# Score tiles of a causal attention in half-array pieces, with the masked quarter of each diagonal block given to another block's scores

## The chip, the cores and the metric

One core of one Trainium2 chip runs the whole program in one launch. The metric is device time in microseconds: 447.69 us, the median of three runs (447.2 to 447.72).

TensorE multiplies matrices into PSUM, here one tile of 8 banks of 128 partitions x 512 fp32. VectorE and ScalarE read PSUM, GpSimd doesn't. SyncE issues most transfers. Each engine works through its own instructions in the order in which the program was written, and semaphores join the engines.

## What is computed

`x` is [1, 2048, 576], bfloat16. The first half of the block is an attention with a compressive memory over four segments of 512 tokens, 32 heads of 18 channels each; the second is a dense layer with GELU, 576 to 4608 and back.

```python
ar = jnp.arange(L)                                   # L = 512
mask = (ar[:, None] < ar[None, :]) * -1000000000.0
for s in range(N):                                   # N = 4 segments
    qs, ks, vs = q[:, :, s], k[:, :, s], v[:, :, s]
    p = _softmax(jnp.einsum('bhqd,bhkd->bhqk', qs, ks) * scale + mask)
    a_dot = jnp.einsum('bhqk,bhkd->bhqd', p, vs)
    pq = phi(qs)
    a_mem = einsum(pq, M) / (einsum(pq, z) + 1e-06)
    outs.append(g * a_mem + (1.0 - g) * a_dot)
    M, z = M + einsum(phi(ks), vs), z + sum(phi(ks))
h = x + attention(_layernorm(x)) @ wo
out = h + gelu(_layernorm(h) @ w1 + b1) @ w2 + b2
```

A query sees only keys at or before it in its segment. So of each 512 x 512 score matrix only the key-query pairs on and below the diagonal count.

## The kernel before

**An order written out by hand.** The program is built as a graph of small operations (`Graph.add`), each with an engine, a cost and a list of those it must follow. A large table, `TIMETABLE`, gives each operation its place: the key is a stage tag and a name ("A1mask": the masks of the attention in segment 1), the letters say which engine (p TensorE, a ScalarE, d VectorE, g GpSimd, s SyncE), and the numbers are places in one order over all engines. `schedule` sorts by these places, hands out buffers, and the instructions are written in that order. So an operation that is not ready holds up all that come behind it on its engine. The costs in `add` are the planner's, used to choose buffers; they are not times of the chip.

**Stages.** X is the first layernorm of a segment, P the three projections, A the attention, M the memory update, B the output projection with the second layernorm, C the first dense product (L1301, in segment 0 L1338), D the second (L1388). TensorE's work of C and D of one segment is laid between that of A of the next. In B, a tile's two halves `Po` and `Ro` run fused (L819, ten matmuls of 128 rows) where they follow each other directly, or else as 10 and 8 matmuls of 64 rows (L793).

**The scores.** A group is four heads; a segment has eight groups. Scores are kept transposed, keys on the partitions and queries along the free axis. Heads have 18 channels, padded to 32, so the four heads of a group use the four 32-row strips of the array at once, each writing its own PSUM bank (`tile_position=(32 * i, 0)`). Key tile `kt` (128 keys) needs queries from `kt * 128` to 512: 512, 384, 256 and 128 columns. A score step fills 512 columns of four banks, and one exponential of 128 x 2048 empties them into a buffer of `pt` (five buffers). In segments 1 to 3 (`stage_A`) five steps serve two groups (`STEPS`): 20 steps a segment, 60 in all, scored at L1163 and exponentiated at L1167. In segment 0 (`stage_A0`) 20 steps are made of other units (L1002, L1005), six of them of four diagonal blocks of 128 columns.

The first 128 columns of every such unit are the diagonal block: half of it is above the diagonal and set to zero by a mask after the exponential. One mask a key tile, by VectorE as a product with a triangle (L1176) or by GpSimd as a select (L1178); in stage 0 two blocks at once (L1015, L1018). The quarter with the upper 64 keys and the lower 64 queries of a diagonal block is void as a whole.

**The values.** Per group, `val` (L1189; L1034 in stage 0) multiplies the four buffers with the values, 16 matmuls on four column tiles of 32, each reading all 128 keys. Then the result is transposed (L1197), divided and combined with the memory's part: `rg` on GpSimd (L1125), `eg` on ScalarE (L1123) and `pq` on VectorE (L1127) make phi(q) in buffers `e` and `r`, and `mem` (L1134 in the full array, L1137 in column tiles) multiplies it.

**Changes of tiling.** Scores use row strips, values column strips, the projections and the first dense product 64-row halves, the rest the full array.

**What else shares the engines.** GpSimd also does rstd of each layernorm (L714, L715), the clips and part of the combining; VectorE and ScalarE share the evictions of PSUM (L630, L634, L1306, L1314, L1316). `warm_up` (L644) runs full-array products of zeros before the first data is there.

Of the kernel before, what the change touches and what calls it, by code (L numbers as in the profile page):

```python
# [318 lines left out]
}  # L319
# [141 lines left out]
def kernel(  # L461
# [11 lines left out]
    nc = tc.nc  # L473
# [1076 lines left out]
```

## Time and profile before

| | |
|---|---|
| time, median of 3 | 447.69 us |
| profiled execution, first to last instruction | 444.7 us |
| TensorE busy | 431.7 us, 97% |
| weight loads | 278.3 us, 63% |
| VectorE, ScalarE, GpSimd busy | 291.2, 296.7, 179.3 us |
| granted TensorE clock | 0.999 |
| exponentials of the scores | 60 of 1.878 us and 20 of 1.880 us |
| score matmuls (L1163, L1002) | 384 and 224 |
| value matmuls (L1189, L1034) | 384 and 224 |

The time is taken around the execution, the span from its first instruction to its last; the profiled execution has only its span. A row of the timeline reads: start, length, engine, line, operation, what it writes and reads, how many, and in brackets the idle time of the engine before it and what ended it. A matmul's length contains the way through the array, so lengths of neighbours overlap: sixteen matmuls that end 0.72 us after their start may let the next one begin after 0.55. A row of the waits reads: who waited, for whom, total, times, longest.

### The profile page before, as it was taken

What the parts mean: (1) busy time and instruction counts of PE and PEld (TensorE: products, weight loads), DVE (VectorE), ACT (ScalarE), POOL (GpSimd) and SP (SyncE); (2) the same over time, 40 slices, a digit from 0 to 9 for tenths busy, and PEclk for the clock granted to TensorE, in tenths of its full rate; (3) what the DMA queues carried; (4) which work ended last, traced back from release to release, by engine and by line L of the source; (5) the groups of instructions that cost most, each with busy time, mean ns of one, the idle gap of its engine ahead of it and who ended that gap; (6) DMA issues with size and microseconds to landing.
All of it is one profiled execution on the core that took longest, in us unless ns stands there. A gap on an engine that the chain in (4) does not pass through costs nothing.

```text
span 444.7 us, 12623 instructions
## 1 busy us (share of the span) xinstructions
PE 431.7 (97%) x5355; PEld 278.3 (63%) x5355; DVE 291.2 (65%) x636; ACT 296.7 (67%) x269; POOL 179.3 (40%) x312
## 2 busy tenths in 40 slices
PE   8888999998999999999999999999999999999997
PEld 5666677765676776664445766654457775446775
DVE  5889888999899988867777987837765121010011
ACT  5999999999878798686798966752684002556000
POOL 5776756457748435734236559440011000000010
PEclk9999999999999999999999999999999999999999
DMA  6779989999999945693863355805463461550030
GB/s 208 204 250 246 271 264 279 228 228 244 236 257 348 315 152 166 175 242 69 245 190 52 107 146 161 201 2 153 131 210 111 101 171 39 169 194 1 1 107 28
DMA packets 85274, 76.73 MB, mean 173 GB/s; under 512 B 62945, under 2 KB 72545, under 8 KB 85217
## 3 DMA queue, kind: packets, MB, share of 16 engines
q1 hardware_dynamic: 85072, 75.83, 63.3%
q8 instruction: 42, 0.69, 0.7%
q10 hardware_dynamic: 144, 0.09, 0.1%
q14 instruction: 16, 0.12, 0.1%
HBM read 42.08 MB, written 18.87 MB: 137 GB/s over the span
## 4 chain that ended last, share of the span: by engine, by line
PE 75%; DVE 7%; DMA 6%; ACT 6%; POOL 2%; issue 2%; SPq 1%; POOLq 0%; DVEq 0%; ACTq 0%
PE bank L1388 27%; PE bank L1301 21%; PE bank L835 9%; PE bank L1338 6%; DMA w1g<-in_B_w_dram 4%; PE bank L1163 3%; ACT hT L1355 3%; PE bank L1189 3%; PE bank L793 2%; DMA x<-in_A_x_dram 2%; ACT pt L1167 1%; PE bank L1002 1%; PE bank L819 1%; DVE ln L710 1%; POOL pt L1178 1%
## 5 line engine op out<-in xcount | busy, mean ns | idle before, releaser
L1167 ACT ACTIVATE pt<-bank 128x2048 bf16<-128x2048 f32 x60 | 112.7, 1878 | 30.4 <-PE bank L1163 25.1
L1388 PEld LDWEIGHTS <-hT 128*128 128x128 bf16 x1152 | 110.2, 98 | 34.5 <-issue 7.0
L1301 PE MATMUL bank<-xreg,w1g 64*128 64x512 bf16 x972 | 108.0, 376 | 0.2 <-DMA w1g<-in_B_w_dram 0.2
L1301 PEld LDWEIGHTS <-w1g 64*128 64x128 bf16 x972 | 46.2, 94 | 57.1 <-issue 2.3
L1388 PE MATMUL bank<-w,hT 128*128 128x288 bf16 x576 | 78.3, 286 | 0.0
L1388 PE MATMUL bank<-w_lo,hT 128*128 128x288 bf16 x576 | 78.0, 286 | 0.0
L835 PE MATMUL bank<-hT,xreg 64*128 64x288 bf16 x864 | 58.0, 283 | 1.1 <-DVE qk_pad L634 0.6
L1306 ACT ACTIVATE hT<-bank,b_col 128x512 bf16<-128x512 f32 x36 | 22.5, 689 | 46.0 <-PE bank L1301 46.0
L1178 POOL TENSOR_SCALAR_AFFINE_SELECT pt<-pt 128x512 bf16<-128x512 bf16 x58 | 42.0, 737 | 27.1 <-ACT pt L1167 26.9
L835 PEld LDWEIGHTS <-xreg 64*128 64x128 bf16 x864 | 41.6, 94 | 14.3 <-issue 5.0
L1400 DVE TENSOR_TENSOR ot<-bank,hc 128x288 bf16<-128x288 f32 x32 | 13.8, 448 | 52.2 <-PE bank L1388 51.1
L1316 DVE TENSOR_SCALAR hT<-bank,b_col 128x512 bf16<-128x512 f32 x49 | 34.9, 742 | 18.6 <-PE bank L1301 18.5
L1374 POOL TENSOR_TENSOR hc<-hc,b_bc 128x576 f32<-128x576 f32 x9 | 11.7, 1297 | 82.0 <-DMA hc<-hd 82.0
L1005 ACT ACTIVATE pt<-bank 128x2048 bf16<-128x2048 f32 x20 | 37.6, 1880 | 2.8 <-PE bank L1002 2.1
L1338 PE MATMUL bank<-xreg,w1g 64*128 64x256 bf16 x648 | 38.3, 269 | 0.6 <-DMA w1g<-in_B_w_dram 0.6
L1338 PEld LDWEIGHTS <-w1g 64*128 64x128 bf16 x648 | 31.3, 94 | 6.4 <-issue 2.7
L1374 DVE TENSOR_TENSOR hc<-hc,b_bc 128x576 f32<-128x576 f32 x7 | 5.6, 817 | 43.8 <-DMA hc<-hd 43.8
L1321 ACT ACTIVATE hT<-hT 128x8192 bf16<-128x8192 bf16 (+2 forms) x6 | 31.8, 5321 | 1.7 <-DVE hT L1316 1.6
L1314 ACT ACTIVATE hT<-bank,b_col 128x512 bf16<-128x512 f32 x23 | 15.1, 685 | 21.9 <-PE bank L1301 21.6
L1176 DVE TENSOR_TENSOR pt<-pt,tri 128x512 bf16<-128x512 bf16 x38 | 21.5, 569 | 4.7 <-ACT pt L1167 4.7
L1163 PE MATMUL bank<-qk 32*128 32x512 bf16 (+3 forms) x384 | 23.8, 300 | 0.2
L1349 DVE TENSOR_TENSOR hT<-bank,b_col 128x512 bf16<-128x512 f32 x32 | 21.0, 681 | 3.8 <-PE bank L1338 3.4
(117 smaller groups left out, 564.1 us busy)
## 6 DMA issues: line engine op xcount, KB each, us to landing
w1g<-in_B_w_dram SPq DMA_DIRECT2D x41, 576.0 KB, 5.0
qkd<-qk_pad SPq DMA_DIRECT2D x15, 512.0 KB, 3.9
hd<-h SPq DMA_DIRECT2D x16, 288.0 KB, 3.9
hc<-hd SPq DMA_DIRECT2D x16, 288.0 KB, 3.6
w_lo<-in_B_w_dram SPq DMA_DIRECT2D x3, 864.0 KB, 7.0
w<-in_B_w_dram SPq DMA_DIRECT2D x3, 864.0 KB, 11.1
xb<-in_A_x_dram SPq DMA_DIRECT2D x16, 144.0 KB, 4.2
x2d<-xn SPq DMA_DIRECT2D x14, 160.0 KB, 2.9
```

The costliest lines, as they stand in the source:

```text
L835: nc.tensor.matmul(out=out, lhsT=xTb.t[r, k, ts], rhs=wt[r, k, :], start=(k == 0), stop=(k == ND - 1))
L1005: ex = add(ps, {"act": 1.88}, lambda e: nc.scalar.activation(out=pt.t[:], in_=st.t[:], func=ACT.Exp, scale=scale), [sc], pt, [st], table=" ...
L1163: nc.tensor.matmul(out=st.t[:, i, off:off + n_], lhsT=qk[rows, 1, kt * P:(kt + 1) * P], rhs=qk[rows, 0, kt * P:L], start=True, stop=True, ...
L1167: ex = add(ps, {"act": 1.88}, lambda e, st=st, pt=pt: nc.scalar.activation(out=pt.t[:], in_=st.t[:], func=ACT.Exp, scale=scale), [sc], pt, ...
L1176: nc.vector.tensor_tensor(out=blk, in0=blk, in1=tri[:].unsqueeze(1).to_broadcast([P, 4, P]), op=ALU.mult)
L1178: nc.gpsimd.affine_select(out=blk, in_=blk, pattern=[[0, 4], [1, P]], compare_op=ALU.is_ge, fill=0.0, base=0, channel_multiplier=-1)
L1301: nc.tensor.matmul(out=cc[w].t[:], lhsT=w1.t[rows, k, q, :], rhs=x2T[s].t[rows, k, :], start=(k == 0), stop=(k == ND - 1))
L1306: ready_f[f + w] = [add(pf - 12, {"act": 0.68}, lambda e, f=f, w=w, cc=cc: nc.scalar.activation(out=hT[:, :, f + w, :], in_=cc[w].t[:].rea ...
L1316: nc.vector.tensor_scalar(out=dst, in0=src, scalar1=b, scalar2=None, op0=ALU.add)
L1321: ge = add(2.9, {"act": 0.42 * (f1 - f0) + 0.2}, lambda e, f0=f0, f1=f1: nc.scalar.activation(out=hT[:, :, f0:f1, :], in_=hT[:, :, f0:f1, ...
L1338: nc.tensor.matmul(out=cc[w].t[:, q * 2 * P:(q + 1) * 2 * P], lhsT=w1.t[rows, k, q, :], rhs=x2T[s].t[rows, k, ts], start=(k == 0), stop=(k ...
L1388: nc.tensor.matmul(out=c.t[:, 0:HALF], lhsT=hT[:, tl // 2, f, (tl % 2) * P:(tl % 2 + 1) * P], rhs=w2_c[ch][:, f - ch * WCH, hf * HALF:(hf ...
```

## The change

- `STEPS` now has nine steps for four groups; each unit is (group, key tile, first query, queries, place). 18 steps a segment.
- `halves` makes each unit of two kinds of matmul, both with 64 keys: one for the lower 64 keys at tile position (32 i, 0), one for the upper at (32 i, 64). For an even key tile, the upper half's first 64 columns, the void quarter, take upper-half-placed scores of the next key tile (its first 64 keys against its first 64 queries); the remaining columns take the unit's own upper keys. The next, odd key tile then leaves out its first 64 queries.
- After the exponential, `drop` copies that quarter, times a triangle, from partitions 64 to 127 to partitions 0 to 63 of a new buffer `low` (one buffer, its upper partitions zero from the start). Only then may `cut` mask the diagonal block, which also zeroes the void quarter. Odd tiles are masked in one operation as two 64 x 64 triangles.
- `val` reads odd key tiles in pieces, the first from `low`: 24 or 28 matmuls a group.
- In stage 0 the six steps of four diagonal blocks are packed likewise into 384 of 512 columns; the two of the first kind keep the quarter in the free columns of their own `pt` buffer.
- `r` has one buffer for two. The warm-up products write other banks. A memset on GpSimd zeroes the upper partitions once.
- The timetable is new throughout: order, and for some operations the engine.

```diff
-    "A1mask": "d456 g466 g515 g495 g474 g547 g537 g545 g620 g585 d572 d602 g645 g633 g643 d616 g661 d681 g672 g674 d705 d686 d712 g713 d744 g757 g756 g762 "
-        "d755 d766 g730 g735",
...
+    low_s = slots(1, [P, 4, P], "low")
...
-    r_s = slots(2, [P, L], "r")
+    r_s = slots(1, [P, L], "r")
...
-        STEPS = [[(0, 0, 0, 512)], [(0, 1, 0, 384), (0, 3, 384, 128)], [(0, 2, 0, 256), (1, 2, 256, 256)],
-                 [(1, 0, 0, 512)], [(1, 1, 0, 384), (1, 3, 384, 128)]]
+        STEPS = [[(0, 0, 0, 512, 0)], [(0, 3, 448, 64, 0), (0, 1, 192, 320, 64), (1, 3, 448, 64, 384), (1, 1, 192, 64, 448)],
+                 [(0, 2, 256, 256, 0), (1, 2, 256, 256, 256)], [(1, 0, 0, 512, 0)], [(1, 1, 256, 256, 0), (2, 1, 256, 256, 256)], [(2, 0, 0, 512, 0)],
+                 [(2, 2, 256, 256, 0), (3, 2, 256, 256, 256)], [(3, 3, 448, 64, 0), (3, 1, 192, 320, 64), (2, 3, 448, 64, 384), (2, 1, 192, 64, 448)],
+                 [(3, 0, 0, 512, 0)]]
...
+        def halves(st, off, n, key, query, k0, q0, k_next, q_next=None):
+            for i in range(4):
+                rows = slice(32 * i, 32 * i + 32)
+                nc.tensor.matmul(out=st.t[0:64, i, off:off + n], lhsT=key(rows, k0, 64), rhs=query(rows, q0, n), start=True, stop=True, tile_position=(32 * i, 0))
+            for c0, c1, k, q in ((0, 64, k_next, q_next or k_next), (64, n, k0 + 64, q0 + 64)) if k_next else ((0, n, k0 + 64, q0),):
+                for i in range(4):
+                    rows = slice(32 * i, 32 * i + 32)
+                    nc.tensor.matmul(out=st.t[64:P, i, off + c0:off + c1], lhsT=key(rows, k, 64), rhs=query(rows, q, c1 - c0), start=True, stop=True,
+                                     tile_position=(32 * i, 64))
...
-            for n in range(5 * (G // 2)):
-                gp, si = divmod(n, 5)
+            for n in range(9 * (G // 4)):
+                gp, si = divmod(n, 9)
...
+                    def below(kt, dg=dg, low=low):
+                        (q0, off, n_, pt, ex), = of_pair[dg, kt]
+                        d0 = 32 * kt
+                        hi = add(ps, {"dve": 0.27, "pool": 0.40}, lambda e: drop(e, low.t[0:64, :, d0:d0 + 64], pt.t[64:P, :, off:off + 64], 1),
+                                 [ex, z_po, ready.get(1)] + later, None if kt else low, [pt] + ([low] if kt else []), name="hi")
+                        mk = add(ps, {"dve": 0.43, "pool": 0.64}, lambda e: cut(e, pt.t[:, :, off:off + P], 1, P), [hi], None, [pt], name="mask")
...
+                        pieces = [(q0, off, n_, pt) for (q0, off, n_, pt, ex) in of_pair[dg, kt]] + ([(kt * P, 32 * (kt - 1), 64, low)] if kt % 2 else [])
```

More of the change, by code (lines that the diff above doesn't have):

```diff
@@ L597, in build @@
     def build():
-        for home in (pad_s, fk_s, xn_s, x_s, xb_s, xT_s, x2_s, oT_s, qk_s, pt_s, h_s, hc_s, ot_s, e_s, r_s, ek_s, rk_s, t1_s, t2_s,
+        for home in (pad_s, fk_s, xn_s, x_s, xb_s, xT_s, x2_s, oT_s, qk_s, pt_s, low_s, h_s, hc_s, ot_s, e_s, r_s, ek_s, rk_s, t1_s, t2_s,
                      xn2_s, on_s, w1_s, ln_s, r1_s, r2_s, c_s):
@@ new lines, in cut @@
+        def cut(e, blk, n, w):
+            src = tri[:, P - w:P].unsqueeze(1).to_broadcast([P, 4, w]) if n == 1 else tri[:, P - w:P].unsqueeze(1).unsqueeze(1).to_broadcast([P, 4, n, w])
+            if e == "dve":
+                nc.vector.tensor_tensor(out=blk, in0=blk, in1=src, op=ALU.mult)
+            else:
+                nc.gpsimd.affine_select(out=blk, in_=blk, pattern=[[0, 4], [1, w]] if n == 1 else [[0, 4], [0, n], [1, w]], compare_op=ALU.is_ge, fill=0.0,
+                                        base=P - w, channel_multiplier=-1)
@@ new lines, in drop @@
+        def drop(e, dst, src, n):
+            if e == "dve":
+                by = tri[64:P, 64:P].unsqueeze(1)
+                nc.vector.tensor_tensor(out=dst, in0=src, in1=by.to_broadcast([64, 4, 64]) if n == 1 else by.unsqueeze(1).to_broadcast([64, 4, n, 64]), op=ALU.mult)
+            else:
+                nc.gpsimd.affine_select(out=dst, in_=src, pattern=[[0, 4], [1, 64]] if n == 1 else [[0, 4], [0, n], [1, 64]], compare_op=ALU.is_ge, fill=0.0,
+                                        base=0, channel_multiplier=-1)
@@ L990, in step @@
                 n += 1
-                st, pt, masks, deps = Buf(c_s, width=4), Buf(pt_s), {}, []
+                packed = len(units) == 4 and units[0][1] * P == units[0][2]
+                st, pt, masks, deps = Buf(c_s, width=4), Buf(pt_s, 1 + Q) if tag == "A00" else Buf(pt_s), {}, []
+                low = Buf(low_s) if packed and tag != "A00" else None
                 lb = [lo_b[2 * Q], lo_b[2 * Q + 1]]
@@ L998, in score @@
                         kk, qq = (qk_lo if kt < 2 else qk_hi), (qk_lo if q0 < 2 * P else qk_hi)
-                        ks, qs = slice((kt % 2) * P, (kt % 2 + 1) * P), slice(q0 % (2 * P), q0 % (2 * P) + n_)
-                        for i in range(4):
-                            rows = slice(32 * i, 32 * i + 32)
-                            nc.tensor.matmul(out=st.t[:, i, off:off + n_], lhsT=kk[rows, 4 * Q + b, 1, ks],
-                                             rhs=qq[rows, 4 * Q + b, 0, qs], start=True, stop=True, tile_position=(32 * i, 0))
@@ L1004, in step @@
-                sc = add(ps, {"pe": 0.28 if len(units) > 2 else 0.24}, score, deps, st, lb, table="rows32", name="st0")
-                ex = add(ps, {"act": 1.88}, lambda e: nc.scalar.activation(out=pt.t[:], in_=st.t[:], func=ACT.Exp, scale=scale),
+                        k0, p0 = (kt % 2) * P, q0 % (2 * P)
+                        if not packed:
+                            for i in range(4):
+                                rows = slice(32 * i, 32 * i + 32)
+                                nc.tensor.matmul(out=st.t[:, i, off:off + n_], lhsT=kk[rows, 4 * Q + b, 1, k0:k0 + P],
+                                                 rhs=qq[rows, 4 * Q + b, 0, p0:p0 + n_], start=True, stop=True, tile_position=(32 * i, 0))
+                            continue
@@ new lines, in score @@
+                        odd = b % 2
+                        halves(st, at[b], n_ - 64 * odd, lambda r, c, n: kk[r, 4 * Q + b + c // L, 1, c % L:c % L + n],
+                               lambda r, c, n: qq[r, 4 * Q + b + c // L, 0, c % L:c % L + n], k0, p0 + 64 * odd, 0 if odd else k0 + L, p0 + L)
+                sc = add(ps, {"pe": 0.34 if packed else 0.28 if len(units) > 2 else 0.24}, score, deps, st, lb, table="rows32", name="st0")
+                cols = slice(0, 384 if packed else 512)
@@ L1006, in step @@
+                ex = add(ps, {"act": 1.47 if packed else 1.88}, lambda e: nc.scalar.activation(out=pt.t[:, :, cols], in_=st.t[:, :, cols], func=ACT.Exp, scale=scale),
                          [sc], pt, [st], table="exp", name="exp")
                 exps.append(ex)
+                if packed:
+                    q64 = lambda r: pt.t[r, :, :].rearrange("p i (b q) -> p i b q", q=64)
+                    hi = add(ps, {"dve": 0.43, "pool": 0.64}, lambda e: drop(
+                        e, low.t[0:64, :, :].rearrange("p i (b q) -> p i b q", q=64) if low else q64(slice(0, 64))[:, :, 6:8, :], q64(slice(64, P))[:, :, 0:8:4, :], 2),
+                             [ex, tri_ok, z_po], low, [pt], name="hi")
+                    m0 = add(ps, {"dve": 0.87, "pool": 1.17}, lambda e: cut(e, pt.t[:].rearrange("p i (b q) -> p i b q", q=256)[:, :, :, 0:P], 2, P), [hi], None, [pt], name="mask")
+                    m1 = add(ps, {"dve": 0.43, "pool": 0.64}, lambda e: cut(e, q64(slice(0, P))[:, :, 2:4, :], 2, 64), [ex, tri_ok], None, [pt], name="mask")
+                    m0.bias, m1.bias = {"dve": MASK_BIAS}, {"dve": MASK_BIAS}
+                    got = []
+                    for (b, kt, q0, n_, off) in units:
+                        got += [(4 * Q + b, kt, q0, 64, 32 * b - 32 + (0 if low else 384), low or pt), (4 * Q + b, kt, q0 + 64, 64, at[b], pt)] if b % 2 else [(4 * Q + b, kt, q0, n_, at[b], pt)]
+                    return got, [m0, m1, hi]
@@ L1151, in stage_A @@
             comb = {}
-            for n in range(5 * (G // 2)):
-                gp, si = divmod(n, 5)
+            for n in range(9 * (G // 4)):
+                gp, si = divmod(n, 9)
                 step = STEPS[si]
                 ps = prio + 0.001 * n
+                if si == 0:
+                    of_pair = {}
                 st, pt = Buf(c_s, width=4), Buf(pt_s)
                 def score(e, st=st, step=step, gp=gp):
-                    for (dg, kt, off, n_) in step:
-                        qk = qks[2 * gp + dg].t
-                        for i in range(4):
-                            rows = slice(32 * i, 32 * i + 32)
-                            nc.tensor.matmul(out=st.t[:, i, off:off + n_], lhsT=qk[rows, 1, kt * P:(kt + 1) * P],
-                                             rhs=qk[rows, 0, kt * P:L], start=True, stop=True, tile_position=(32 * i, 0))
-                gs = sorted({2 * gp + u[0] for u in step})
-                sc = add(ps, {"pe": 0.23}, score, [qk_ok[g] for g in gs], st, [qks[g] for g in gs], table="rows32", name="st")
+                    for (dg, kt, q0, n_, off) in step:
+                        qk = qks[4 * gp + dg].t
+                        halves(st, off, n_, lambda r, c, n: qk[r, 1, c:c + n], lambda r, c, n: qk[r, 0, c:c + n], kt * P, q0, 0 if kt % 2 else (kt + 1) * P)
+                gs = sorted({4 * gp + u[0] for u in step})
+                sc = add(ps, {"pe": 0.30 if len(step) == 2 and step[0][1] == 2 else 0.27 if len(step) == 1 else 0.24}, score, [qk_ok[g] for g in gs], st,
+                         [qks[g] for g in gs], table="rows32", name="st")
                 ex = add(ps, {"act": 1.88}, lambda e, st=st, pt=pt: nc.scalar.activation(out=pt.t[:], in_=st.t[:], func=ACT.Exp, scale=scale),
@@ L1169, in stage_A @@
                 exps.append(ex)
-                for (dg, kt, off, n_) in step:
-                    g = 2 * gp + dg
-                    def mask(e, pt=pt, off=off):
-                        blk = pt.t[:, :, off:off + P]
-                        if e == "dve":
-                            nc.vector.tensor_tensor(out=blk, in0=blk, in1=tri[:].unsqueeze(1).to_broadcast([P, 4, P]), op=ALU.mult)
-                        else:
-                            nc.gpsimd.affine_select(out=blk, in_=blk, pattern=[[0, 4], [1, P]], compare_op=ALU.is_ge, fill=0.0,
-                                                    base=0, channel_multiplier=-1)
-                    mk = add(ps, {"dve": 0.45, "pool": 0.67}, mask, [ex] + later, None, [pt], name="mask")
-                    mk.bias = {"dve": MASK_BIAS}
-                    vops.setdefault(g, []).append((kt, off, n_, pt, mk))
+                for (dg, kt, q0, n_, off) in step:
+                    of_pair.setdefault((dg, kt), []).append((q0, off, n_, pt, ex))
@@ new lines, in stage_A @@
+                if si < 8:
+                    continue
+                for dg in range(4):
+                    low, ready = Buf(low_s), {}
+                    def below(kt, dg=dg, low=low):
[4 more added lines that the diff above has]
+                        mk = add(ps, {"dve": 0.43, "pool": 0.64}, lambda e: cut(e, pt.t[:, :, off:off + P], 1, P), [hi], None, [pt], name="mask")
+                        mk.bias = {"dve": MASK_BIAS}
+                        ready[kt] = mk
+                        ready[kt + 1] = hi
+                    below(0)
+                    (q0, off, n_, pt, ex), = of_pair[dg, 3]
+                    mo = add(ps, {"dve": 0.43, "pool": 0.64}, lambda e, pt=pt, off=off: cut(e, pt.t[:, :, off:off + P].rearrange("p i (b q) -> p i b q", q=64), 2, 64),
+                             [ex] + later, None, [pt], name="mask")
+                    mo.bias = {"dve": MASK_BIAS}
+                    below(2)
+                    for kt in range(4):
+                        pieces = [(q0, off, n_, pt) for (q0, off, n_, pt, ex) in of_pair[dg, kt]] + ([(kt * P, 32 * (kt - 1), 64, low)] if kt % 2 else [])
+                        vops.setdefault(4 * gp + dg, []).append((kt, pieces, [ready[kt]] + [u[4] for u in of_pair[dg, kt]] + ([mo] if kt % 2 else [])))
@@ L1186, in vals @@
                 def vals(e, g=g):
-                    for (kt, off, n_, pt, _) in sorted(vops[g], key=lambda v: v[0]):
-                        for i in range(4):
-                            nc.tensor.matmul(out=ox[g].t[32 * i:32 * i + Dh + 1, kt * P:L], lhsT=va[kt][:, 4 * g + i, :], rhs=pt.t[:, i, off:off + n_],
-                                             start=kt == 0, stop=kt == 3, tile_position=(0, 32 * i), skip_group_check=True)
-                comb[g] = add(prio + 0.1 + 0.001 * (5 * (g // 2) + 3 * (g % 2)), {"pe": 0.56}, vals, [z_va[s], [v[4] for v in vops[g]], [v_ok[s, kt, g // 4] for kt in range(TPS)]],
-                              ox[g], [v[3] for v in vops[g]], table="cols32", name="val")
+                    for (kt, pieces, _) in sorted(vops[g], key=lambda v: v[0]):
+                        for (c0, off, n_, pt) in pieces:
+                            for i in range(4):
+                                nc.tensor.matmul(out=ox[g].t[32 * i:32 * i + Dh + 1, c0:c0 + n_], lhsT=va[kt][:, 4 * g + i, :], rhs=pt.t[:, i, off:off + n_],
+                                                 start=kt == 0, stop=kt == 3, tile_position=(0, 32 * i), skip_group_check=True)
+                comb[g] = add(prio + 0.1 + 0.001 * (5 * (g // 2) + 3 * (g % 2)), {"pe": 0.59}, vals, [z_va[s], [v[2] for v in vops[g]], [v_ok[s, kt, g // 4] for kt in range(TPS)]],
+                              ox[g], list(dict.fromkeys(u[3] for v in vops[g] for u in v[1])), table="cols32", name="val")
             done = []
@@ L1411, in build, with zero_po @@
         PE_FLIP_X, PE_X, PE_QK = (0,), ((0, 0), (0, 1), (1, 0)), (0, 1)
+        gr.tag = "Z"
+        def zero_po(e):
+            for u in low_s.tiles:
+                VEC[e].memset(u[64:P, :, :], 0.0)
+            for u in pt_s.tiles[1:3]:
+                VEC[e].memset(u[64:P, :, 384:512], 0.0)
+        z_po = add(0.2, {"dve": 0.9, "pool": 2.0}, zero_po, (), name="memset")
         stage_X(0, 0.0)
```

7 lines of the change are left out of this document (4 added, 3 removed), and 590 rows, old and new, of the table TIMETABLE.

## The prediction

> **What bounds the kernel now.** I read the page's first part and its chain first, then the busy time by stretches, then who made TensorE wait.
>
> ```profile
> PE 431.7 (97%) x5355; PEld 278.3 (63%) x5355; DVE 291.2 (65%) x636; ACT 296.7 (67%) x269; POOL 179.3 (40%) x312
> PE 75%; DVE 7%; DMA 6%; ACT 6%; POOL 2%; issue 2%; SPq 1%; POOLq 0%; DVEq 0%; ACTq 0%
> ```
>
> ```profile
> 15.00:45.00 30.00, 27.07 (x565) 20.20 (x558) 27.71 (x71) 27.88 (x42) 21.66 (x35) 1.00 0.93 247
> 45.00:85.00 40.00, 40.00 (x764) 30.01 (x762) 35.30 (x81) 37.50 (x32) 24.20 (x64) 1.00 1.04 255
> 85.00:190.00 105.00, 101.72 (x1478) 69.51 (x1474) 95.30 (x210) 89.22 (x76) 63.83 (x97) 1.00 0.89 237
> 190.00:300.00 110.00, 109.68 (x1164) 61.74 (x1158) 80.92 (x163) 84.94 (x56) 53.98 (x80) 1.00 0.54 142
> ```
>
> The columns after the length are the busy microseconds of TensorE, its weight loads, VectorE, ScalarE and GpSimd. From 15 to 300 us, the stretch that holds all of the attention, TensorE is idle for 2.93 + 0.00 + 3.28 + 0.32 = 6.5 us of 285; ScalarE is 93% and 94% busy in the first two rows, 85% and 77% in the next two. So the end is set by the sum of TensorE's work, and by 6.5 us of idle time between its instructions; the loaded vector engines count only through those gaps. Who ends them:
>
> ```profile
> PE bank L1002 <- DVE xreg L634: 0.9, 1, 0.9
> PE bank L1134 <- DVE t L1197: 0.8, 1, 0.8
> PE bank L1002 <- ACT pt L1005: 0.8, 2, 0.6
> PE bank L835 <- DVE qk_pad L634: 0.6, 1, 0.6
> ...
> PE bank L1189 <- POOL pt L1178: 0.3, 1, 0.3
> ...
> PE bank L1189 <- DVE pt L1176: 0.2, 1, 0.2
> ```
>
> Each is a single late producer, none repeats by the dozen. Masks (L1178, L1176) delay the value matmuls by only 0.5 us in all.
>
> **What a score step and a value step cost TensorE.** The matmuls overlap, so I read prices from start to start, not from durations.
>
> ```profile
> 187.11 0.40 PE L1163 MATMUL bank<-qk 32*128 32x512 bf16 x4
> 187.44 0.91 PE L1388 MATMUL bank<-w_lo,hT 128*128 128x288 bf16 x6
> ...
> 218.59 0.72 PE L1189 MATMUL bank<-pt,v_aug 128*19 128x512 bf16 x16
> 219.14 0.39 PE L1137 MATMUL bank<-e,MZ_blk 128*32 128x512 bf16 x4
> ...
> 248.12 0.72 PE L1189 MATMUL bank<-pt,v_aug 128*19 128x512 bf16 x16
> 248.78 0.40 PE L1163 MATMUL bank<-qk 32*128 32x512 bf16 x4
> ```
>
> Sixteen value matmuls stream 512 + 384 + 256 + 128 = 1280 columns, four column tiles side by side. Followed by the same tiling they take 0.55 us (219.14 - 218.59), followed by another 0.66. So a column costs 0.55 / 1280 = 0.43 ns, a change of tiling 0.11 us, and a score step of 512 columns 0.33 us (187.44 - 187.11), which is 0.22 of streaming and one change.
>
> **Score steps, stages 1 to 3.** Five steps for two groups become nine for four: 60 steps become 54. Each half of the array now streams 512 columns, the lower and the upper half of the keys side by side. If the halves run at once, a step still costs 0.33: 54 x 0.33 = 17.8 for 60 x 0.33 = 19.8, **-2.0 us**. But a unit with an even key tile loads its upper half twice, 64 columns of the next key tile first and then its own. There are 8 such units in nine steps, 48 in all. No 64-column matmul stands in the trace. The nearest rows are 128-column ones:
>
> ```profile
> 17.41 0.41 PE L1002 MATMUL bank<-qk 32*128 32x128 bf16 x16 [0.19 <-ACT pt L1005]
> 17.74 5.69 PE L835 MATMUL bank<-hT,xreg 64*128 64x288 bf16 x90
> ...
> 28.59 0.85 PE L1034 MATMUL bank<-pt,v_aug 128*19 128x128 bf16 x48
> 29.37 0.68 PE L738 MATMUL bank<-ident,xn 128*128 128x128 bf16 x9
> ```
>
> ```profile
> L1163 PEld LDWEIGHTS <-qk 32*128 32x128 bf16 x384 | 7.0, 92 | 15.3 <-issue 14.8 <-DMA hd<-h 0.2 <-DMA xreg<-x2d 0.2
> ```
>
> Sixteen matmuls in fours of 128 columns cost 0.33 us, no more than four of 512, and 48 of them 0.78, against 1536 x 0.43 ns + 0.11 = 0.77: weights that change every 55 ns (128 columns) are hidden. Over 64 columns (0.027 us) a load of 0.092 us can stick out by 0.065. Bounds 0 and 0.065 a reload; as the rows sit at the cheap end I take 0.03: 48 x 0.03 = **+1.4** (0 to +3.1).
>
> **Diagonal steps of stage 0.** Six of its 20 steps stream 384 columns a half for 512, 0.055 us less each, with 2 reloads each: 6 x (0.06 - 0.055) = **0.0** (-0.3 to +0.5).
>
> **Value steps.** The columns stay, but a group has 24 or 28 matmuls for 16, because a tile's first 64 columns now lie in another buffer: 60 more quads in stages 1 to 3, 12 in stage 0. From nothing (the 48 above) to 0.065 each; I take 0.015, as most stand beside a long quad: **+1.1** (0 to +4.7).
>
> **The order on TensorE.** Reading both timetables as orders, I count its changes of tiling: 210 before, 202 after. Six of the eight went with the six steps; two more are 2 x 0.11 = **-0.2**. Of the sixteen output projections four ran fused before (L819, 40 matmuls of ten each) and two do now:
>
> ```profile
> 244.22 0.49 PE bank L793 x8
> ...
> 252.95 1.23 PE bank L819 x10
> ...
> 321.23 0.61 PE bank L793 x10
> ```
>
> Split costs 0.61 + 0.49 = 1.10, fused 1.23: 2 x -0.13 = **-0.3**. TensorE's work: -2.0 + 1.4 + 0 + 1.1 - 0.2 - 0.3 = **0.0 us** (bounds -2.8 to +5.8).
>
> **The other engines** reach the end only through the gaps.
>
> ```profile
> L1167 ACT ACTIVATE pt<-bank 128x2048 bf16<-128x2048 f32 x60 | 112.7, 1878 | 30.4 <-PE bank L1163 25.1 <-DVE pt L1176 1.4 <-issue 1.4
> L1005 ACT ACTIVATE pt<-bank 128x2048 bf16<-128x2048 f32 x20 | 37.6, 1880 | 2.8 <-PE bank L1002 2.1 <-POOL ln L715 0.3 <-PE bank L1034 0.2
> L1123 ACT ACTIVATE e<-qk 128x512 bf16<-128x512 bf16 x24 | 14.9, 626 | 0.3 <-PE bank L1137 0.2
> L1178 POOL TENSOR_SCALAR_AFFINE_SELECT pt<-pt 128x512 bf16<-128x512 bf16 x58 | 42.0, 737 | 27.1 <-ACT pt L1167 26.9
> L1176 DVE TENSOR_TENSOR pt<-pt,tri 128x512 bf16<-128x512 bf16 x38 | 21.5, 569 | 4.7 <-ACT pt L1167 4.7
> L1424 POOL TENSOR_SCALAR_AFFINE_SELECT tri<-tri 128x128 bf16<-128x128 bf16 x1 | 0.3, 294 | 0.1
> ```
>
> ScalarE loses 6 x 1.878 = 11.3 us, and in six stage-0 steps 512 of 2048 elements at (1878 - 626) / 1536 = 0.82 ns, 6 x 0.42 = 2.5; both timetables give it 254 operations, so six others, mostly evictions of a product's bank, come back to it. The masks: 96 of 128x512 become 72 and 48 triangles of 64x256 into the separate tile, by the timetable 47 and 36 of them on GpSimd (58 before), 25 and 12 on VectorE (38). A 256-element select lies at 0.44 us between the rows for 128 and 512. GpSimd: -11 x 0.737 + 36 x 0.44 = +7.7 us; VectorE: -13 x 0.569 + 12 times something under 0.57, -7.4 to -0.6. GpSimd has room (64 of 105 us). One new memset of three 64x512 pieces opens GpSimd's queue:
>
> ```profile
> 3.45 0.83 POOL L610 MEMSET qk_pad<- 128x896 bf16 x1
> ```
>
> about 3 x 0.5 us by elements, ahead of the two pad memsets, the gate and the identity. The x load covers it; uncovered, the first transposes start up to 1.5 us late.
>
> Of the 6.5 us of gaps I give back **1.5**. The 2.5 us of ScalarE's saving that fall in stage 0 come where it is 93% busy, and 0.8 us of waits name its exponentials there; most other waits are of VectorE, which gets little relief of its own but shares evictions with ScalarE. Bounds: 4 of them go, or 4 come in (the mask rival below). Sum: 0.0 - 1.5 = -1.5 us. The profiled span is 444.7 us, 3.0 less than the median of 447.69 for what lies around it; so the span becomes 443.2 and the **time 446.2 us**.
>
> **The rivals.** (a) **The mask chain (slower).** A value step now waits for exponential, then triangle copy, then mask of the same block (two steps where one was), and the only copy tile is held from a group's first copy to its value matmuls. Behind a waiting copy on GpSimd stand masks, clips and the layernorms' rstd, and value matmuls hold up all of TensorE. In the order, 12 of 24 value steps follow their last mask or copy with no TensorE work between, 9 before. Against it: of those 9 only some waited, 0.5 us in all, and the least TensorE work between a group's last exponential and its values is about 2.3 us after, 2.1 before. It decides from 1.5 / 12 = 0.13 us on each of the 12; at 0.3 (two thirds of a copy) and no gap won it costs 3.6: 447.7 + 3.6 = 451.3. (b) **Small matmuls at their bounds (slower).** Reloads and extra quads at 0.065: +3.1 + 4.7 + 0.5 for 2.5 taken, +5.8: 452.0 with the gaps as forecast. The 128-column rows speak against it. (c) **The halves do not run at once (slower).** Then each step streams 0.22 more: 54 x 0.22 + 6 x 0.165 = 12.9, 459.1. For it: no row shows row and column tiles mixed. Against it: the sixteen value matmuls share all four row groups and still ran four abreast. The Trainium skill, "TensorE: Matmul & The Clock Gate", Part 3, says that weight loads overlap matmuls in flight only when the row group differs; both halves of a step share theirs, so by that rule alone (c) would hold, but the value rows disagree with it as it stands. (d) **Nothing shows**: work even and the same gaps, 447.7. (e) **ScalarE was the hidden limit**: 4 us of gaps go and the reloads hide, 447.7 - 4 - 1.4 = 442.3.
>
> **Chances.** Forecast 43% (its own range 444.7 to 447.3), (a) 24%, (b) 9%, (c) 6%, (d) 10%, (e) 8%. About 0.2%, 0.9 us, can be told from no change. Faster by more: 41 of the forecast's 43 and (e), with 1 of (a) left over: 50%. Same: (d), the forecast's 2 and 4 of (a): 16%. Slower: 34%. The range goes from (e) past (a) and (b), 441.5 to 453.5, and leaves out (c) and the tails of (a) and (b).
>
> **What would show it.** Right: score steps at about 0.33 to 0.40 us from start to start, value steps within 0.1 us of 0.55 or 0.66, tiling changes as counted, TensorE idle near 5 us between 15 and 300 us, ScalarE's exponentials 54 in number and 14 us shorter. Wrong: score steps at 0.55 (c); many waits of value matmuls on masks, GpSimd and the copy tile (a); value steps at 0.9 (b); idle time in the first 20 us behind GpSimd's memsets.

## The result, and the profile after

The change makes the kernel slower: 449.26 us against 447.24 (medians of nine runs each), a ratio of 1.0052 with a 95% interval of 1.0029 to 1.0075. Its times also scatter more, 447.74 to 452.81 where those of before lie between 446.62 and 448.01. The two slowest runs show a granted TensorE clock below 0.999, 0.996 at 450.78 us and 0.992 at 452.81; the median run has 0.999, so the loss itself does not come from the clock. 446.2 had been forecast; the time lies in the range, on the other side.

First the page of the kernel after, its busy times and its chain, then the exponentials and copies in its groups:

```profile
PE 433.8 (97%) x6478; PEld 288.1 (64%) x6478; DVE 294.1 (66%) x646; ACT 286.8 (64%) x271; POOL 180.9 (40%) x331
PE 83%; DVE 8%; POOL 5%; issue 2%; DMA 1%; ACT 0%; SPq 0%; POOLq 0%; DVEq 0%; ACTq 0%
```

```profile
L1224 ACT ACTIVATE pt<-bank 128x2048 bf16<-128x2048 f32 x54 | 101.3, 1877 | 39.6 <-PE bank L971 28.5 <-POOL low L987 2.8 <-PE bank L1259 2.8
L1050 ACT ACTIVATE pt<-bank 128x2048 bf16<-128x2048 f32 x14 | 26.3, 1880 | 2.8 <-PE bank L1042 2.6
L987 POOL TENSOR_SCALAR_AFFINE_SELECT low<-pt 64x256 bf16<-64x256 bf16 x36 | 16.0, 450 | 25.4 <-PE bank L1259 15.2 <-ACT pt L1224 8.6 <-POOL pt L979 0.4
L1050 ACT ACTIVATE pt<-bank 128x1536 bf16<-128x1536 f32 x6 | 8.7, 1454 | 1.8 <-PE bank L971 1.7
```

The exponentials fall by 14.0 us (101.3 + 26.3 + 8.7 against 112.7 + 37.6), as worked out, and ScalarE's share of the chain falls from 6% to nothing. TensorE is the bound as before, with 1123 more pairs of weight load and matmul. What a step costs it, in its timeline: one value step followed by the same tiling, one full score step, and one value step followed by another tiling.

```profile
210.71 0.53 PE L1259 MATMUL bank<-pt,v_aug 128*19 128x512 bf16 x12
211.07 0.20 PE L1259 MATMUL bank<-low,v_aug 128*19 128x64 bf16 x4
211.10 0.31 PE L1259 MATMUL bank<-pt,v_aug 128*19 128x256 bf16 x8
211.24 0.20 PE L1259 MATMUL bank<-low,v_aug 128*19 128x64 bf16 x4
211.27 0.39 PE L1194 MATMUL bank<-e,MZ_blk 128*32 128x512 bf16 x4
...
217.99 0.41 PE L967 MATMUL bank<-qk 32*64 32x512 bf16 x4
218.00 0.41 PE L971 MATMUL bank<-qk 32*64 32x64 bf16 x8
218.35 2.12 PE L1371 MATMUL bank<-xreg,w1g 64*128 64x512 bf16 x18
...
220.40 0.53 PE L1259 MATMUL bank<-pt,v_aug 128*19 128x512 bf16 x12
220.76 0.20 PE L1259 MATMUL bank<-low,v_aug 128*19 128x64 bf16 x4
220.79 0.31 PE L1259 MATMUL bank<-pt,v_aug 128*19 128x256 bf16 x8
220.92 0.20 PE L1259 MATMUL bank<-low,v_aug 128*19 128x64 bf16 x4
221.06 0.41 PE L967 MATMUL bank<-qk 32*64 32x512 bf16 x4
```

Twelve half-array matmuls take 0.36 us from start to start (a row counts together matmuls that differ in columns), where four whole ones took 0.33; 28 value matmuls take 0.56 and 0.66, where 16 took 0.55 and 0.66. So the halves run at once, and small matmuls are almost free. Only the six packed steps of segment 0 are clearly dearer: 0.46 us for their 40 matmuls (the second starts at 20.48 us and what follows it at 20.94), where the 16 of a step of four diagonal blocks took 0.33.

The time went elsewhere. Who made TensorE wait, in the kernel after:

```profile
PE bank L1408 <- issue: 1.1, 1, 1.1
PE bank L1091 <- POOL pt L979: 0.9, 1, 0.9
PE bank L842 <- DVE v_aug L641: 0.8, 1, 0.8
...
PE bank L842 <- issue: 0.5, 1, 0.5
...
PE bank L1259 <- issue: 0.4, 1, 0.4
```

"issue" is idle time for which the profile shows no releaser. Before, TensorE had no such row. The three places in the timeline:

```profile
33.19 0.78 PE L842 MATMUL bank<-hT,xreg 64*128 64x288 bf16 x6
34.46 0.79 PE L842 MATMUL bank<-hT,xreg 64*128 64x288 bf16 x10 [0.49 <-issue]
...
146.44 0.19 PE L1259 MATMUL bank<-low,v_aug 128*19 128x64 bf16 x1
147.00 0.20 PE L1259 MATMUL bank<-low,v_aug 128*19 128x64 bf16 x3 [0.37 <-issue]
...
152.66 0.81 PE L1408 MATMUL bank<-xreg,w1g 64*128 64x256 bf16 x11
154.56 0.61 PE L1408 MATMUL bank<-xreg,w1g 64*128 64x256 bf16 x8 [1.09 <-issue]
```

Each lies inside a run of matmuls of one operation, between two that read the same tiles. From start to start they cost 0.75, 0.56 and 1.34 us beyond the usual interval, 2.65 together. Counted through the trace from 0, the stopped matmuls are number 607, 2911 and 3039 of the program: 128 x 4, 22 and 23, plus 95. And in the queues of the two pages, before first, the one that loads instructions has grown with the pairs:

```profile
q8 instruction: 42, 0.69, 0.7%
...
q8 instruction: 50, 0.82, 0.8%
```

50 packets of 16 KB where 42 stood before; 50 x 128 = 6400 pairs of 6478, and 42 x 128 = 5376 of 5355. So a packet holds 128 of TensorE's pairs; the stops divide the program into the same blocks. What that queue did between the last two stops, from two stretches of the transfer view (queue, kind: packets, MB, share of the 16 engines):

```profile
q1 hardware_dynamic: 1456, 1.92, 114.2%
```

```profile
q1 hardware_dynamic: 1484, 1.82, 113.0%
q8 instruction: 1, 0.02, 1.1%
```

The first is the stretch from 145.6 to 151.9 us, the second from 147 to 153.2: in both the transfer engines are full, in the first no packet of instructions comes through, in the second one. By its own times it began at 151.98 and landed at 153.05; TensorE had begun the block before at 147.00, was through with it at 153.2, and went on at 154.56. The stop at 146.44 is alike: landed 145.57, on at 147.00. So is the first: landed 33.09, on at 34.46. **A block's first matmul comes no sooner than about 1.4 us after its packet landed, and at the three stops that packet began only 3.2, 3.4 and 5.0 us after the first matmul of the block before.** When it is asked for, the trace does not show. The Trainium skill, "Runtime: NRT & Kernel Launch", "Instruction fetch mechanics", says that instructions come in blocks of 16 KiB, 256 instructions, through a transfer queue of the sequencer's own, and that the cost of a block boundary is mostly hidden. By that rule the stops would be near zero. The trace agrees on the block (128 loads and 128 matmuls) and not on the cost.

### The profile page after: what moved, and what is told of

It is laid out like the page before. It is cut to its first block, busy times and chain, and to the rows that moved or that the text cites. A ratio compares the mean times of both kernels' runs of the same rounds, so it can differ in the third digit from the quotient of the medians.

```text
span 447.4 us, 14961 instructions
## 1 busy us (share of the span) xinstructions
PE 433.8 (97%) x6478; PEld 288.1 (64%) x6478; DVE 294.1 (66%) x646; ACT 286.8 (64%) x271; POOL 180.9 (40%) x331
## 4 chain that ended last, share of the span: by engine, by line
PE 83%; DVE 8%; POOL 5%; issue 2%; DMA 1%; ACT 0%; SPq 0%; POOLq 0%; DVEq 0%; ACTq 0%
PE bank L1458 31%; PE bank L1371 24%; PE bank L842 9%; PE bank L1408 5%; PE bank L800 4%; PE bank L1259 3%; PE bank L967 3%; DVE hT L1419 2%; PE bank L971 2%; DMA x<-in_A_x_dram 1%; POOL pt L979 1%; DVE xn L733 1%; PE bank L1191 1%; DVE e L1184 1%; PE bank L745 1%
## 5 line engine op out<-in xcount | busy, mean ns | idle before, releaser
L1224 ACT ACTIVATE pt<-bank 128x2048 bf16<-128x2048 f32 x54 | 101.3, 1877 | 39.6 <-PE bank L971 28.5
L842 PE MATMUL bank<-hT,xreg 64*128 64x288 bf16 x864 | 59.6, 283 | 2.3 <-DVE v_aug L641 0.8
L979 POOL TENSOR_SCALAR_AFFINE_SELECT pt<-pt 128x512 bf16<-128x512 bf16 (+1 forms) x58 | 44.0, 767 | 23.0 <-DVE low L985 15.7
L1376 ACT ACTIVATE hT<-bank,b_col 128x512 bf16<-128x512 f32 x36 | 22.4, 690 | 45.6 <-PE bank L1371 45.4
L1386 DVE TENSOR_SCALAR hT<-bank,b_col 128x512 bf16<-128x512 f32 x43 | 31.1, 742 | 11.9 <-PE bank L1371 11.3
L1050 ACT ACTIVATE pt<-bank 128x2048 bf16<-128x2048 f32 (+1 forms) x20 | 35.0, 1752 | 4.6 <-PE bank L1042 2.6
L1384 ACT ACTIVATE hT<-bank,b_col 128x512 bf16<-128x512 f32 x29 | 19.1, 683 | 20.5 <-PE bank L1371 20.3
L987 POOL TENSOR_SCALAR_AFFINE_SELECT low<-pt 64x256 bf16<-64x256 bf16 (+1 forms) x39 | 18.4, 476 | 26.1 <-PE bank L1259 15.2
L721 POOL TENSOR_SCALAR ln<-ln 128x1 f32<-128x1 f32 x32 | 8.6, 268 | 44.2 <-DVE ln L718 42.1
L967 PE MATMUL bank<-qk 32*64 32x256 bf16 (+4 forms) x496 | 24.2, 271 | 0.6 <-ACT pt L1050 0.5
L971 PE MATMUL bank<-qk 32*64 32x64 bf16 (+4 forms) x720 | 24.6, 238 | 0.0
```

What stands on the lines that cost most here:

```text
L842: nc.tensor.matmul(out=out, lhsT=xTb.t[r, k, ts], rhs=wt[r, k, :], start=(k == 0), stop=(k == ND - 1))
L967: nc.tensor.matmul(out=st.t[0:64, i, off:off + n], lhsT=key(rows, k0, 64), rhs=query(rows, q0, n), start=True, stop=True, tile_position=(3 ...
L971: nc.tensor.matmul(out=st.t[64:P, i, off + c0:off + c1], lhsT=key(rows, k, 64), rhs=query(rows, q, c1 - c0), start=True, stop=True, tile_p ...
L979: nc.gpsimd.affine_select(out=blk, in_=blk, pattern=[[0, 4], [1, w]] if n == 1 else [[0, 4], [0, n], [1, w]], compare_op=ALU.is_ge, fill=0 ...
L1050: ex = add(ps, {"act": 1.47 if packed else 1.88}, lambda e: nc.scalar.activation(out=pt.t[:, :, cols], in_=st.t[:, :, cols], func=ACT.Exp, ...
L1224: ex = add(ps, {"act": 1.88}, lambda e, st=st, pt=pt: nc.scalar.activation(out=pt.t[:], in_=st.t[:], func=ACT.Exp, scale=scale), [sc], pt, ...
```

## The experiments

To read a trace I add TensorE's intervals from one matmul's start to the next one's, taking an interval with idle time in it at its usual length; what is over is idle. Before: 428.6 us of work and 10.9 idle; after: 429.7 and 13.0, of which 2.65 at block boundaries. The sums, 439.5 and 442.7, and the stops are firm; where work ends and idle time begins moves by about 1 us with what is taken as usual.

**Odd key tiles whole.** Steps that hold only odd key tiles have the same queries in both halves, so whole tiles do:

```diff
                     for (dg, kt, q0, n_, off) in step:
                         qk = qks[4 * gp + dg].t
+                        if kt % 2:
+                            for i in range(4):
+                                rows = slice(32 * i, 32 * i + 32)
+                                nc.tensor.matmul(out=st.t[:, i, off:off + n_], lhsT=qk[rows, 1, kt * P:(kt + 1) * P], rhs=qk[rows, 0, q0:q0 + n_],
+                                                 start=True, stop=True, tile_position=(32 * i, 0))
+                            continue
```

> The changed kernel, with the steps that hold only odd key tiles (three of nine) scored by whole 32x128 tiles, 4 matmuls a unit for 8: 240 pairs of weight load and matmul fewer, nothing else moved. Fetch theory (TensorE's instructions come in blocks of 128 pairs; a block can start no sooner than about 1.4 us after its 16 KB transfer landed, and TensorE stops where 128 pairs are done before that): stops with no semaphore behind them fall from 2.7 us in the profile to under 1.5, time 447.0 to 448.5 us. Mask theory (value steps wait for the two-step masks and the one copy tile): no change, 449.3. Work theory (small matmuls cost more than the columns they stream): 448.7 to 449.0, the steps concerned each up to 0.1 us shorter.

448.33 us, ratio to before 1.0027 (1.0010 to 1.0044), half the loss of the change, though its interval overlaps the change's. Two boundary stops of 0.85 us each are left in its profile, 1.7 in all, more than the 1.5 expected; score work falls by 0.6 us. It supports the fetch theory without deciding.

**The kernel before, cut in pieces.** Score and value matmuls of segments 1 to 3 in pieces of 128 columns, in the old order with the old masks (the score part; the value part is cut alike):

```diff
-                        for i in range(4):
-                            rows = slice(32 * i, 32 * i + 32)
-                            nc.tensor.matmul(out=st.t[:, i, off:off + n_], lhsT=qk[rows, 1, kt * P:(kt + 1) * P],
-                                             rhs=qk[rows, 0, kt * P:L], start=True, stop=True, tile_position=(32 * i, 0))
+                        for c in range(0, n_, P):
+                            for i in range(4):
+                                rows = slice(32 * i, 32 * i + 32)
+                                nc.tensor.matmul(out=st.t[:, i, off + c:off + c + P], lhsT=qk[rows, 1, kt * P:(kt + 1) * P],
+                                                 rhs=qk[rows, 0, kt * P + c:kt * P + c + P], start=True, stop=True, tile_position=(32 * i, 0))
```

> The kernel before, with score and value matmuls of segments 1 to 3 cut into pieces of 128 columns: 1152 pairs more (the change added 1123), same columns, same order, same masks. Fetch theory: stops at places that lie 128 pairs apart appear, 1.5 to 5 us in all, time 449 to 452 us and a wider spread than before's 1.4 us. Mask theory: nothing, 447.2. Work theory: each of 288 further quads costs up to 0.015 us evenly spread, no stops, 447.5 to 451.

449.68 us, 1.0051 (1.0035 to 1.0068): the change's whole loss, with nothing of the change but its number of pairs. The spread did not widen (449.50 to 450.54 in six runs), against the expectation. Its timeline:

```profile
139.85 0.34 PE L1164 MATMUL bank<-qk 32*128 32x128 bf16 x10
141.59 0.28 PE L1164 MATMUL bank<-qk 32*128 32x128 bf16 x6 [1.40 <-issue]
```

One score step is torn after its tenth matmul, for 1.6 us; the next is number 2655 = 128 x 20 + 95. Two more stops of 0.7 stand at the blocks beside it (134.5 and 147.1). The three come to 2.9 of the 3.6 us by which this profile is longer than before's. Its work is 428.7 us, as before's 428.6: 288 further quads (four matmuls side by side) cost about 0.1 us in all.

**Short masks.** The triangle copies and masks of segments 1 to 3 on 2 columns (parts of the lines; the masks of the last key tiles alike):

```diff
-... drop(e, low.t[0:64, :, d0:d0 + 64], pt.t[64:P, :, off:off + 64], 1) ...
+... drop(e, low.t[0:64, :, d0:d0 + 2], pt.t[64:P, :, off:off + 2], 1, 2) ...
...
-... cut(e, pt.t[:, :, off:off + P], 1, P) ...
+... cut(e, pt.t[:, :, off:off + 2], 1, 2) ...
```

> The changed kernel, with the triangle copies and masks of segments 1 to 3 cut to 2 columns each (the rest of the triangles is left out, so the values are not masked): same instructions, order and waits, each short. Mask theory: 2 us or more faster than the change, 447 or less. Fetch theory: the stops at block boundaries stay, 448.3 to 449.5.

448.87 us, 1.0027 (1.0005 to 1.0049), no sooner than 447, so masks do not carry the loss. Its profiled run has boundary stops of up to 2.8 us:

```profile
140.81 1.00 PE L935 MATMUL bank<-v_aug,fk_pad 128*128 128x76 bf16 x24
144.44 0.43 PE L935 MATMUL bank<-v_aug,fk_pad 128*128 128x76 bf16 x8 [2.62 <-issue]
```

Without boundary stops its idle time is about 9.2 us, where the change's is 10.3 in both its profiles: up to about 1 us may be the masks'. The intervals overlap, so that stays open.

**Less traffic.** Two kernels of the change with parts of the dense layer's weights not loaded (parts of the lines; the products read the loaded part):

```diff
-... w2_c[c][:])[1], lambda c=c: B_w2[c * P:(c + 1) * P, :].rearrange("p (f d) -> p f d", d=D), 740e3 ...
+... w2_c[c][:, 0:1 if c > 2 else WCH, :])[1], lambda c=c: B_w2[c * P:(c + 1) * P, :].rearrange("p (f d) -> p f d", d=D)[:, 0:1 if c > 2 else WCH, :], 740e3 ...
...
-... w1.t[:].rearrange("p k q m -> p (k q m)"), lambda fg=fg: B_w1[fg * P:(fg + 1) * P, :], 520e3 ...
+... w1.t[:, 0:1 if s == 0 else ND, :, :].rearrange("p k q m -> p (k q m)"), lambda fg=fg: B_w1[fg * P:(fg + 1) * P, 0:2 * P * (1 if s == 0 else ND)], 520e3 ...
```

The first edit alone:

> The changed kernel, with the last three of six loads of the second dense weights cut to a sixth (the products of those chunks all read the loaded sixth): same instructions, about 2.2 MB less traffic, which fell at 143 to 156 us. Fetch theory with transfers as what delays the fetch: the stops at 146 and 153 us (0.56 and 1.36 us) go or shrink below 0.3, time 447.3 to 448.5. If the fetch is late for another reason, or masks or work are to blame: 449.0 to 449.5.

448.33 us, 1.0029 (1.0013 to 1.0046). Its profiled run is the slowest of its twelve (451.13 us). In it the stops at 146 and 153 us had shrunk as expected, but 2.0 us at 143.7, 1.9 at 137.3 and 1.3 at 60 stood in their place: ahead of the stretch that this edit relieves. Both edits:

> The changed kernel with all its instructions, the last three loads of the second dense weights cut to a sixth and the 14 loads of the first dense weights for segment 0 cut to a ninth (those products read the loaded part; the rest is left out): about 9 MB less traffic between 20 and 160 us. If busy DMA engines are what delays the fetch: stops under 0.5 us each, time 446.5 to 448, spread under 2 us. If the fetch is late whatever the traffic: stops of 1 to 2 us stay, 449.

447.52 us, 1.0002 (0.9988 to 1.0016), 447.12 to 448.18 in twelve runs. All instructions of the change are there, and its loss is gone with the traffic, its scatter too. The share of the 16 transfer engines between 20 and 160 us fell from 1.00 to 0.83. The profile is 2.0 us shorter than the change's (445.4 for 447.4 us) and its stops are 1.8 us shorter, so the lighter traffic gained next to nothing elsewhere. One issue row is left, the first stop:

```profile
32.95 0.78 PE L842 MATMUL bank<-hT,xreg 64*128 64x288 bf16 x6
34.31 0.91 PE L842 MATMUL bank<-hT,xreg 64*128 64x288 bf16 x12 [0.58 <-issue]
```

Over six profiles (before, after and the four kernels up to the first light one) I set 291 packets of the instruction queue beside how busy the 16 transfer engines were around the start of the block before, from 1 us ahead of it to 3 us after:

```
transfer engines busy   packets   begins after that block's first matmul: mean, most
under 30%               68        -1.0 us    0.8 us
30 to 70%               64        -0.1       3.9
70 to 100%              62         1.3       5.2
over 100%               97         1.6       5.3
```

The packet itself takes 1.1 to 1.2 us on average in each row, though single ones took up to 2.5: that one lies ahead of the second stop of the kernel with whole odd tiles. So what is late is mostly the packet's start, and it is late where other transfers are dense. (Shares over 100% come from packets that overlap on an engine.)

**Fewer pairs at the same columns.** The first dense product of segment 0 by one matmul of 512 columns for two of 256, which leaves out half of that product's weights:

```diff
-                        for q in range(2):
-                            for k in range(ND):
-                                for w in range(2):
-                                    rows = slice(64 * w, 64 * w + 64)
-                                    nc.tensor.matmul(out=cc[w].t[:, q * 2 * P:(q + 1) * 2 * P], lhsT=w1.t[rows, k, q, :], rhs=x2T[s].t[rows, k, ts],
-                                                     start=(k == 0), stop=(k == ND - 1))
+                        for k in range(ND):
+                            for w in range(2):
+                                rows = slice(64 * w, 64 * w + 64)
+                                nc.tensor.matmul(out=cc[w].t[:].rearrange("p (q t) -> p q t", q=2), lhsT=w1.t[rows, k, 0, :],
+                                                 rhs=x2T[s].t[rows, k, ts].unsqueeze(1).to_broadcast([64, 2, 2 * P]), start=(k == 0), stop=(k == ND - 1))
```

In the kernel before:

> The kernel before, with the first dense product of segment 0 done by one matmul of 512 columns (the same 256 tokens twice) for two of 256 with different weights; half of that product's weights are left out. 324 pairs fewer, all between 20 and 160 us, as many columns. Both theories: no stops at block boundaries before or after, only the saved pairs' overhead, 18 runs of 36 matmuls at 2.07 us become 18 matmuls at about 1.97 (a 512-column pair of the later product takes 0.219 us): 1.8 us faster, 445.0 to 446.0 us. It is the base for the next kernel.

446.63 us, 0.9980 (0.9967 to 0.9994). It gained 0.5 us, not 1.8: that product's work went from 37.3 to 37.1 us, so halving the pairs saves next to nothing by itself. In the change:

> The changed kernel with the same edit. Fetch theory: the fewer pairs also take away most of the stops, so it gains 3 us or more, to 445.5 to 446.5, and stands 0 to 1 us behind the kernel before with this edit, where the change stood 2.0 behind. Work or masks: it gains the 1.8 us alone and stays 2.0 behind, 447.3 to 447.6.

447.39 us, 0.9996 (0.9981 to 1.0011), 446.60 to 447.92: 0.8 us behind the kernel before with the same edit, where the change was 2.0 behind. The time is later than the 446.5 expected at most, as the edit gained less in the kernel before too; the distance came out as the fetch theory said. The one stop left is again that at 34 us, 0.75. With the odd tiles whole as well:

> The changed kernel with that edit and with the odd steps in whole tiles, 564 pairs fewer in all. Fetch theory: no stop longer than 0.3 us; equal to the kernel before with the edit within 0.5 us, that is, with fetch out of the way the change is worth nothing either way. If it is 1 us or more faster than that one, fetch hid a gain of the change; if 1 us or more slower, something other than fetch costs time.

446.76 us, 0.9993 (0.9978 to 1.0009): 0.1 us from the kernel before with the edit. One stop of 0.5 us is left, at 33.5, where none over 0.3 had been expected. With fetch nearly out of the way the change is worth nothing, either way.

**The change again**, unaltered:

> The changed kernel unaltered, for a second profile and more times on one chip. Fetch theory: where a fetch lands depends on what else is in the transfer queues, so the stops without a semaphore differ from the first profile in place and length, but each one lies at the same distance within a block of 128 pairs; their sum is 1 to 4 us, and the time minus that sum is 446 to 447.5 us in both profiles. Another theory of a fixed late producer: the same stops at the same places. Median 448.5 to 449.5.

449.80 us, 1.0049 (1.0028 to 1.0070), 447.47 to 451.76. Its profile against the first one's 152.66 and 154.56:

```profile
153.33 0.92 PE L1408 MATMUL bank<-xreg,w1g 64*128 64x256 bf16 x13
155.34 0.92 PE L1408 MATMUL bank<-xreg,w1g 64*128 64x256 bf16 x13 [1.09 <-issue]
```

The same three blocks stop, 0.89, 1.08 and 1.34 us, and two more by 0.2 each. So the places did not move as I had expected; the lengths did. The time less the stops is 446.5 us in the first profile and 445.9 in this one, just under the 446 expected. A place that stays, on which I had set the two theories against each other, was no test. Two other findings are. Of the 20 idle times of 0.2 us or more that nine profiles with stops put to issue, all lie at 95 within a block of 128. And over all eleven profiles 23 matmuls at such a place start more than 0.5 us after the one before; each does so 1.26 to 1.56 us after its packet landed, and no block of any profile starts sooner after its own than that.

No version that leaves nothing out was faster than the kernel before.

## Why the prediction was wrong

**TensorE bounds the kernel, ScalarE's saving does not count by itself:** right. 14 us less on ScalarE gave back at most the waits counted below.

**Score steps:** 54 at 0.33 with 0.03 a reload, 19.2 us for 19.8, were expected. They took 0.36 to 0.37 each, 19.6 us for 19.9, and those of odd key tiles alone, which reload nothing, took as long as the others; in whole tiles they took 0.33 again. So the 0.03 came out by luck: it is a price of the halves, one a step, and not of a reload. **Diagonal steps of segment 0:** 0.0 expected, at most +0.5; six at 0.46 for 0.33 are +0.8, a term out of its bounds. All score work went from 26.5 to 26.9 us. **Value steps:** +1.1 expected, +0.7 measured (19.7 to 20.4). Work as a whole was put at 0.0 and is +1.1 of 428.6 by this count.

**The gaps: this step failed.** I gave back 1.5 of 6.5 us because ScalarE would be less late. The same stretches after:

```profile
15.00:45.00 30.00, 27.35 (x713) 20.15 (x712) 26.24 (x65) 25.93 (x40) 22.87 (x41) 1.00 0.93 209
45.00:85.00 40.00, 39.07 (x774) 29.45 (x774) 36.90 (x87) 35.48 (x32) 21.63 (x54) 1.00 0.94 263
85.00:190.00 105.00, 100.97 (x1928) 73.54 (x1924) 90.90 (x201) 82.28 (x74) 68.29 (x117) 1.00 0.92 240
190.00:300.00 110.00, 109.96 (x1619) 66.39 (x1613) 88.85 (x185) 84.98 (x60) 48.31 (x78) 1.00 0.60 143
```

TensorE is idle for 2.65 + 0.93 + 4.03 + 0.04 = 7.65 us, of which 0.49 + 0.37 + 1.09 = 1.95 stand at the three stops; the other 5.7 are 0.8 us less than before, half of what I took. But I priced each added instruction by the array's time and none by what it takes to bring it in: that term was put at nothing without a reason. 128 pairs passed in 8.4 us on average between 85 and 160 us before (1143 matmuls in 75 us), and in 6.3 after (1515), and 2.65 to 3.7 us of stops came in. From start to start over the whole profile the sum is +1.1 - 0.5 + 2.65 = 3.2 us, less 0.5 for TensorE's earlier first matmul (1.24 us for 1.78): the span's 2.7. How much of it is work and how much is waiting depends on the count; that the two and the earlier start together come to about zero, and the stops to the rest, does not.

That the time lies in the range is luck: its slow side was set by (a) and (b), and neither is what happened.

**The rivals.** None of the five was this one. (c), the halves one after the other, is out by the 0.36; (b), small matmuls at their bounds, by the value steps' +0.7 us for its +4.7, though the six packed steps did pass their bound; (a), the mask chain, is at most about 1 us of it. The case that nothing shows, (d), would hold without the fetch: 446.76 against 446.63. (e), that ScalarE was the hidden limit, fell: 0.8 us of gaps went, not 4. The rule against the change that I weighed, on weight loads of one row group, did not bite; the fetch page I did not weigh.

## What to carry to other kernels

Count TensorE's instructions, not only its columns. The latest packets here began 5.3 us after the block before, took 1.1 on average, and the block came 1.4 after that: an estimate of 7.8 us for the slowest fetch under dense transfers. Where TensorE passes 128 pairs of weight load and matmul in less, it can stop, here for up to 2.8 us, with no semaphore behind it. Not every such block stops: in the kernel before 12 of 41 pass in less, and none does. A stop "on issue" in the middle of one operation's matmuls, at a constant place modulo 128, is that. Cutting matmuls finer is almost free on the array (288 more quads cost about 0.1 us) only where such fetches are early.

## What was not expected of the hardware

A block of TensorE's instructions was fetched only about one block ahead: its packet began on average 1.0 us before the first matmul of the block ahead of it where transfers were few, and as late as 5.3 us after it where they were dense; of 524 packets in eleven profiles none began more than 2.7 us before it. From landing to the first matmul took about 1.4 us (1.37, 1.43 and 1.51 at the three stops). The same page of the Trainium skill gives TensorE room for eight such blocks; in no run here did the fetch run so far ahead.

A granted clock of 0.992 to 0.996 came up in 11 of 69 runs of the change, its repeat and four of its variants (odd tiles whole, short masks, the first light one, wide with odd tiles whole), and in none of 123 runs of the kernel before and of the other four. No experiment here asks why.
